# Query loads in halves, key pieces that skip three slots and a later raw block, in a block-sparse attention and MLP kernel

## The chip, the cores and the metric

The kernel runs on one core of a Trainium2 chip. The metric is the time of one execution in microseconds (us), as the median over runs. PE is TensorE's matmul side and PEld its weight loads, DVE is VectorE, ACT is ScalarE, POOL is GpSimd, and SP is SyncE, which here only issues DMAs. "SPq" and "POOLq" are the sides of SP and POOL that issue. A KB of the profile is 1024 bytes; a kB here is 1000.

## The reference

Four batches of eight heads, 768 tokens in 24 blocks of 32, head size 64. Each block of queries sees its own block, its two neighbours, the first and the last block, and three sampled blocks; the first and the last block of queries see everything ("dense"). The result goes through a two-layer MLP.

```python
scores = scale * np.matmul(q, k.transpose(0, 1, 3, 2))
mask = np.abs(blk_i - blk_j) <= 1
mask = mask | (blk_i == 0) | (blk_j == 0) | (blk_i == n_blocks - 1) | (blk_j == n_blocks - 1)
for qb in range(n_blocks):
    for kb in sampled_blocks[qb]:
        mask[qb * block:(qb + 1) * block, kb * block:(kb + 1) * block] = True
scores = np.where(mask, scores, -1000000000.0)
attn = softmax(scores)
x = np.matmul(attn, v)            # reshaped to 3072 tokens x 512
r = np.maximum(x @ w_in, 0.0)     # 512 -> 2048
out = (s * (r * r) + b) @ w_out   # 2048 -> 512
```

## The kernel before, in words

**Attention (about the first 245 us).** Batches 0 and 1 form pair 0, batches 2 and 3 pair 1. The list `T["ORD"]` gives 'slots' in the order of the work. Pair 0 begins with four dense slots (0 to 3); then three streams take turns, C, A and B: slot 4 is the first of C, 5 of A, 6 of B, 7 the second of C, and so on. C walks blocks 17 to 22, A blocks 1 to 8, B blocks 16 down to 9. Pair 1 does the same after four more dense slots that are strewn among the last slots of pair 0. A sparse slot handles one block of queries for all heads of two batches. On PE it is 64 score matmuls (`s`, line 953), 8 transposes of the probabilities (`t`, line 1010), 64 products with the values (`xs`, line 1062), and two transposes of the result (line 1074); every third slot adds products for the dense rows (`od`, line 1052). DVE takes maxima (line 970), ACT the exponentials (line 982).

**What a slot loads.** SP issues the slot's window values (`vA`, line 781) and its three sampled values (line 875), 128 KB each, and stores the result of an earlier slot (`xd<-xst`, line 1086). POOL copies the window's key block and the three sampled key blocks from the pair's key tile `kt` into the work tile `kk` (lines 892 and 903); it does so three slots ahead, as soon as PE has read the stream's previous slot.

**Queries.** A query tile `qr` holds four blocks of queries of two batches, 512 KB, and comes in four DMAs of 128 KB: `load_q` (line 712), two for each batch `a`. A stream changes tile after four slots. In the trace they are called qr_4s and qr_5s (C), qr_0s and qr_1s (A), qr_3s and qr_2s (B) for the sparse slots of either pair, and qr_0d for the dense slots. POOL issues the sparse ones between its key copies; SP issues the dense ones. Four tiles are held at a time.

**Keys of pair 1.** They come in 12 pieces (`key_piece`, `load_k`, line 695), 256 KB each, one right behind the sampled values of each of the slots 9 to 20 (`"K1": 9`).

**Weights.** `w_in` and `w_out` come as 64-bit words and are decoded on DVE, ACT and POOL (lines 85 to 95). The first six blocks (`T["WL"]`: i0 o0 i1 o1 i2 i3) are loaded in two halves of 256 KB each (lines 59 and 62) and decoded during the attention of pair 1; their due time is `wat`, 14 units apart, where a sparse slot has four units.

**What sets the order.** Every step is registered with a cost, a due time and what it needs (`op`). `Plan.order` then lays the steps out on a modelled time axis, with a modelled DMA queue, and the program is written in that order, engine by engine. So a change of due times or of explicit predecessors (`order=`) can move other steps too. On the chip each engine runs its own list in that order.

**MLP (from about 246 us).** PE multiplies without a break: line 617 and the lines 438 to 440 (first layer), 480 to 482 (second).

The lines that the change touches: the table `T` (line 29), `queries` (lines 1160 to 1173), the branch for sparse slots (1181 to 1195), the key pieces (1214) and `wat` (1348).

Of the kernel before, what the change touches and what calls it, by code (L numbers as in the profile page):

```python
# [212 lines left out]
def kernel(  # L213
# [31 lines left out]
    KPS = (4, 12)  # L245
# [415 lines left out]
    with ExitStack() as es:  # L661
# [467 lines left out]
        def key_piece(e, a, p, prio, order=()):  # L1129
            nonlocal prev_k  # L1130
            prev_k = op("s", 450, prio, lambda: load_k(e, a, p), alloc=[] if p or a else [(f"kt{e}", e)],
                        use=[(f"kt{e}", e)] if p or a else [], order=[prev_k, *order], nbytes=3146e3 / KPS[e] / (1 if e else 2))
            for y in range(2) if a is None else (a,):
                kld[(e, y, p)] = prev_k
# [15 lines left out]
        first_pk = first_q = pq = pvl = pvs = pk = o_m = o_e = o_rc = o_ev = None  # L1150
        spills, tensor, lqs, before, globs = {}, {}, {}, {}, {}

        costs = {"s": (530, 470, 265), "d": (810, 350, 780)}
        cols = {"s": (1800, 1024, 500), "d": (1536, 768, 768)}
        for i, (kind, e, k, r) in enumerate(slots):
# [3 lines left out]
            qk = q_of(i)  # L1159
            def queries():  # L1160
                nonlocal pq, first_q
                if qk in lqs:
                    return
                if not dense:
                    first_q = first_q or qk
                lqs[qk] = {}
                for a in range(2):
                    for par in range(2):
                        fresh = not (a or par)
                        pq = op("s" if dense else "g", 450 if dense else 700, max(u - T["QL"], -18.0 if dense else -4.5) + 0.01 * par + (9.5 * (u == 0) if dense else 0.02) * a,  # L1170
                                lambda qk=qk, a=a, par=par: load_q(qk, a, par), alloc=[("qr", qk)] if fresh else [], use=[] if fresh else [("qr", qk)],
                                order=[pq] if dense else [pq, o_rg if first_q in (None, qk) else first_pk], nbytes=131e3)
                        lqs[qk].setdefault(a, []).append(pq)
# [6 lines left out]
            else:  # L1180
                prev = before.get(r)
                entire = k == STREAMS[r]
                first = not before
# [5 lines left out]
                first_pk = first_pk or pk  # L1189
                queries()  # L1190
                for a in range(NSL):
                    pk = op("g", 460, u - T["GK"] + 0.1 * (a + 1), lambda i=i, a=a: sampled_k(i, a), [o_rg, *parts_of(e, range(NB))],
                            alloc=[] if a else [("kg", i)], use=[(f"kt{e}", e), ("kk", "kk")] + ([("kg", i)] if a else []), order=[pk])
                    s_deps.append(pk)
                s_use += [("kk", "kk"), ("kg", i)]

# [16 lines left out]
                pv_at.append((u, pvs))  # L1213
                if 0 <= i - T["K1"] < KPS[1]:
                    key_piece(1, None, i - T["K1"], u - T["GV"] + 0.4, [pvs])
                av_use = [*vt, ("vs", i)]
# [129 lines left out]
        for k, (which, f) in enumerate((w[0], int(w[1:])) for w in T["WL"].split()):  # L1346
            load, st = decode(which, f, k)
            wat = N + min(T["WP"] + T["WS"] * k, T["WE"] + T["WD"] * k if k < 6 else 1e9)
            raw, wp = ("kraw", (which, f)), (f"wp{quarter_of(k)}", (which, f))
# [218 lines left out]
```

## Time and profile before

| | |
|---|---|
| three runs | 772.94, 774.55 and 776.96 us, median 774.55 us |
| the profiled execution | 772.34 us, its span 770.6 us |
| busy, of the span | PE 732.4 us, DVE 568.1 us, ACT 475.1 us, POOL 242.1 us |
| instructions on PE | 8032 matmuls, 8032 weight loads |
| mean granted clock of PE | 0.986 |
| DMA | 89.14 MB, 116 GB/s over the span |
| key pieces of pair 1 issued | from 44.3 to 95.9 us |

The profile comes from one execution. Its page has busy times by engine, the span in 40 slices, DMA queues, and the chain of work that ended last, followed back from the last instruction. Other views are the waits (who waited for whom: sum, count, longest), stretches ("windows": for each engine the busy time and the count of instructions, then PE's granted clock, the DMA engines' busy share and GB/s), a tile's instructions, and the chain and the timeline in order of time (start, duration, what). "issue" is time in which an engine waited for nothing that the profile shows.

### The profile page before, as it was taken

The page shows a single profiled execution, that of the slowest core. Times are in us where ns is not written, and L with a number is a line of the kernel's source. Part 1 is how long each engine was busy: PE and PEld are TensorE (multiplying, and loading weights), DVE is VectorE, ACT ScalarE, POOL GpSimd, SP SyncE. Part 2 cuts the span into 40 slices and gives each one's busy share as a digit, 9 for nine tenths or more (in the row PEclk, how much of TensorE's full clock was granted, in tenths as well). Part 3 has the DMA queues.
Part 4 walks back from the last instruction along what each step waited for, and adds up shares of the span by engine and source line. Part 5 has one row for each costly group of instructions (what it writes and reads, how often), then busy time and mean ns, then how long its engine had stood idle before and what let it go on. Part 6 is the DMA issues. An engine that isn't in the chain of part 4 may idle for free.

```text
span 770.6 us, 21377 instructions
## 1 busy us (share of the span) xinstructions
PE 732.4 (95%) x8032; PEld 619.7 (80%) x8032; DVE 568.1 (74%) x1437; ACT 475.1 (62%) x1143; POOL 242.1 (31%) x398
## 2 busy tenths in 40 slices
PE   8699898999788999999989999999999999999997
PEld 6377675676567999999878998888998998888896
DVE  4767466988586789897896688687678678667652
ACT  3767576888586878789753444565443567344433
POOL 4936244546230221211022232223222232222221
PEclk9989999999899999999999999999999999999999
DMA  8978888877774534635433222224000022000002
GB/s 237 235 199 223 233 215 223 206 202 213 178 202 117 159 110 148 209 118 161 101 126 90 76 83 75 63 69 123 1 1 1 1 62 83 1 1 0 1 1 82
DMA packets 100998, 89.14 MB, mean 116 GB/s; under 512 B 50208, under 2 KB 79520, under 8 KB 100896
## 3 DMA queue, kind: packets, MB, share of 16 engines
q1 hardware_dynamic: 98592, 81.50, 37.8%
q0 software_dynamic: 2304, 6.29, 3.3%
q8 instruction: 63, 1.03, 0.6%
q14 instruction: 39, 0.32, 0.1%
HBM read 68.89 MB, written 14.68 MB: 108 GB/s over the span
## 4 chain that ended last, share of the span: by engine, by line
PE 75%; DVE 9%; ACT 5%; issue 4%; DMA 3%; POOL 1%; SPq 1%; POOLq 0%; ACTq 0%; DVEq 0%
PE m L617 20%; PE o L481 10%; PE o L482 10%; PE o L480 10%; PE xs L1062 5%; PE s L953 5%; PE t L1010 4%; PE h L438 3%; PE h L440 2%; PE h L439 2%; PE od L1052 2%; DVE ptile L970 1%; PE xs L1074 1%; DMA qr_3s<-in_q_dup_dram 1%; DVE xp L601 1%
## 5 line engine op out<-in xcount | busy, mean ns | idle before, releaser
L459 POOL TENSOR_TENSOR hid<-hid,hid 128x384 fp32r<-128x384 f32 x96 | 105.6, 1101 | 292.3 <-ACT hid L635 245.6
L634 ACT ACTIVATE hid<-hid,sb_b,sb_s 128x384 f32<-128x384 f32 x96 | 68.0, 709 | 151.6 <-DVE hid L628 151.5
L982 ACT ACTIVATE ptile<-ptile,nm 128x256 f32<-128x256 f32 (+1 forms) x208 | 107.2, 518 | 35.3 <-DVE nm L970 35.0
L970 DVE CUSTOM_DVE_ANT_1 ptile<-s,mt 128x256 f32<-128x256 f32 x176 | 64.4, 421 | 33.2 <-PE s L953 32.4
L482 PE MATMUL o<-woutr,hid 128*128 128x512 f32 x168 | 66.4, 395 | 0.0
L481 PE MATMUL o<-woutr,hid 128*128 128x512 f32 x168 | 66.3, 395 | 0.0
L480 PE MATMUL o<-woutr,hid 128*128 128x512 f32 x168 | 65.3, 389 | 0.0
L617 PE MATMUL m<-wout,win 128*128 128x384 f32 x264 | 62.6, 340 | 2.1 <-ACT xrest L1461 1.6
L617 PE MATMUL m<-xp,wop 128*128 128x384 f32 x288 | 58.3, 337 | 0.0
L1062 PEld LDWEIGHTS xs<-vA,pt 128*32 128x32 f32 x1696 | 36.6, 113 | 26.9 <-issue 8.5
L481 PE MATMUL o<-win,hid 128*128 128x512 f32 x144 | 56.8, 395 | 0.0
L628 DVE SCALAR_TENSOR_TENSOR hid<-hid 128x384 f32<-128x384 f32 x96 | 54.3, 566 | 3.3
L1010 PE MATMUL t<-ident,ptile 128*128 128x128 f32 x352 | 51.0, 285 | 5.7 <-issue 5.3
L617 PE MATMUL m<-xp,win 128*128 128x384 f32 x288 | 55.1, 338 | 1.4 <-DVE xp L601 0.7
L1062 PE MATMUL xs<-vA,pt 128*32 128x64 f32 x1696 | 49.0, 228 | 6.5 <-issue 5.3
L617 PEld LDWEIGHTS m<-xp,win 128*128 128x128 f32 x288 | 50.9, 188 | 4.5 <-DVE xp L601 1.2
L635 ACT CAST hid<-hid 128x384 fp32r<-128x384 f32 x96 | 49.4, 514 | 7.5 <-PE o L482 0.4
L617 PEld LDWEIGHTS m<-xp,wop 128*128 128x128 f32 x288 | 51.5, 188 | 2.1
L617 PEld LDWEIGHTS m<-wout,win 128*128 128x128 f32 x264 | 47.4, 188 | 5.1 <-ACT xrest L1461 2.5
L482 PE MATMUL o<-win,hid 128*128 128x512 f32 x126 | 49.8, 395 | 0.0
L892 POOL COPY kk<-kt 128x256 f32<-128x256 f32 (+2 forms) x46 | 21.3, 466 | 90.4 <-PE s L953 90.2
L480 PE MATMUL o<-win,hid 128*128 128x512 f32 x126 | 49.2, 391 | 0.2
(191 smaller groups left out, 1860.6 us busy)
## 6 DMA issues: line engine op xcount, KB each, us to landing
vB<-in_v_dram SPq DMA_DIRECT2D x113, 128.0 KB, 4.1
vA<-in_v_dram SPq DMA_DIRECT2D x73, 128.0 KB, 3.9
raw_o<-in_w_out_dram SPq DMA_DIRECT2D x14, 512.0 KB, 3.4
raw_i<-in_w_in_dram SPq DMA_DIRECT2D x12, 512.0 KB, 3.8
xd<-xst SPq DMA_DIRECT2D x44, 128.0 KB, 3.7
out_dram<-ob SPq DMA_DIRECT2D x20, 256.0 KB, 2.0
sum<-xd SPq DMA_DIRECT2D x12, 384.0 KB, 4.2
kt<-in_k_blk_dram SPq DMA_DIRECT2D x8, 384.0 KB, 5.5
```

Of the source, the lines that this page charges most:

```text
L459: (eng or nc.vector).tensor_tensor(out=htile(5 + i % 3), in0=t, in1=gh.bitcast(F32), op=ALU.subtract)
L480: nc.tensor.matmul(acc, gh[:, tsl], wout(f, 0), start=first, stop=False)
L481: nc.tensor.matmul(acc, gh[:, tsl], wout(f, 1), start=False, stop=False)
L482: nc.tensor.matmul(acc, gl[:, tsl], wout(f, 0), start=False, stop=last)
L617: nc.tensor.matmul(to, w_, x_, start=(c == 0 and k == 0), stop=(c == 1 and k == 2))
L628: vec.scalar_tensor_tensor(out=t, in0=t, scalar=0.0, in1=t, op0=ALU.max, op1=ALU.mult)
L634: nc.scalar.activation(t, t, AF.Identity, bias=sb_b, scale=sb_s)
L635: nc.scalar.copy(gh, t)
L970: nc.vector.tensor_tensor_reduce(out=pt, in0=sp, in1=msk, scale=-scale, scalar=FMAX if g == 0 else nm[:, 0:1], op0=ALU.add, op1=ALU.min, a ...
L982: nc.scalar.activation(pt[:, :w], pt[:, :w], AF.Exp, bias=nms[n][:, last:last + 1], scale=-1.0, accum_out=dns[i][:, g, j:j + 1])
L1010: nc.tensor.transpose(tp[:, (2 * j + c) * P:(2 * j + c + 1) * P], src[:, c * P:(c + 1) * P], ident)
L1062: nc.tensor.matmul(xs[quads[pair]], pt[:, c, quads[pair]], vt[:, a, col:col + D], start=(j == 0 and c == 0), stop=(c == 1), tile_position= ...
```

## The change

Three edits, and what the planner makes of them. First, the query loads of the second tile of streams A and B may come in two halves, one for each batch: `queries` takes the halves it shall load and a predecessor. Second, the 12 key pieces of pair 1 go behind the sampled values of slots 6 to 14 and 18 to 20 instead of 9 to 20, so slots 15, 16 and 17 have none and slots 6, 7 and 8 have one. Third, the due time of weight block number 4 (i2) is 6 units later.

```diff
-    ... "K1": 9, ...
+    ... "K1": (6, 7, 8, 9, 10, 11, 12, 13, 14, 18, 19, 20), ...
...
-            def queries():
+            def queries(which=(0, 1), after=None):
                 nonlocal pq, first_q
-                if qk in lqs:
+                if which[0] in lqs.setdefault(qk, {}):
                     return
...
-                lqs[qk] = {}
-                for a in range(2):
+                for a in which:
...
-                                order=[pq] if dense else [pq, o_rg if first_q in (None, qk) else first_pk], nbytes=131e3)
+                                order=[pq] if dense else [pq, after, o_rg if first_q in (None, qk) else first_pk], nbytes=131e3)
...
                 prev = before.get(r)
+                if qk[2] == 1:
+                    queries((0,), lastk[sorted(lastk)[-2]])
+                    queries((1,), pk)
+                elif qk[2] == 2:
+                    queries((0,), pk)
...
-                queries()
+                if qk[2] != 2:
+                    queries()
...
+                queries((1,), pk)
+                lastk[i] = pk
...
-                if 0 <= i - T["K1"] < KPS[1]:
-                    key_piece(1, None, i - T["K1"], u - T["GV"] + 0.4, [pvs])
+                if i in T["K1"]:
+                    key_piece(1, None, T["K1"].index(i), u - T["GV"] + 0.4, [pvs])
...
-            wat = N + min(T["WP"] + T["WS"] * k, T["WE"] + T["WD"] * k if k < 6 else 1e9)
+            wat = N + min(T["WP"] + T["WS"] * k, T["WE"] + T["WD"] * k + 6.0 * (k == 4) if k < 6 else 1e9)
```

On POOL, at the place where stream B of pair 1 gets its second query tile, before (qr_1s and qr_2s are query tiles, kk<-kt the key copies of one slot, wklp<-raw_o a step of a weight's decoding):

```order
L712 DMA qr_1s<-in_q_dup_dram 64x4x128 x4
...
L712 DMA qr_2s<-in_q_dup_dram 64x4x128 x4
L88 COPY wklp_549<-raw_o_3745 128x512
L892 COPY kk<-kt_753 128x256
...
L892 COPY kk<-kt_753 128x256
```

and the same place now:

```order
L712 DMA qr_1s<-in_q_dup_dram 64x4x128 x4
...
L712 DMA qr_2s<-in_q_dup_dram 64x4x128 x2
L88 COPY wklp_551<-raw_o_3745 128x512
L892 COPY kk<-kt_465 128x256
...
L712 DMA qr_2s<-in_q_dup_dram 64x4x128 x2
L892 COPY kk<-kt_465 128x256
```

Two of the four loads of qr_2s stand behind the key copies of one more slot. The four of qr_1s stand together as they did. Pair 0 shows the same two changes, and its four loads of the next qr_4s now stand together, behind the copies of slot 21, where three stood behind those of slot 22 and one behind those of slot 23.

On SP, early in pair 0, behind the sampled values of slot 6 (vA, vB are value tiles, kt the key pieces), before:

```order
L875 DMA vB<-in_v_dram 32x2x512
L781 DMA vA<-in_v_dram 96x2x512
L872 DMA vB<-in_v_dram 32x2x512
L875 REGISTER_ALU
```

and now:

```order
L875 DMA vB<-in_v_dram 32x2x512
L695 DMA kt_465<-in_k_blk_dram 128x2x256
L781 DMA vA<-in_v_dram 96x2x512
L872 DMA vB<-in_v_dram 32x2x512
L875 REGISTER_ALU
```

A key piece stands ahead of the next value loads; two more follow behind slots 7 and 8. Later on SP, the three pieces behind slots 15, 16 and 17 are gone, and three of the four loads of qr_0d for pair 1's dense slots move forward by one to two slots, so that three of them now stand among the key pieces of slots 18 to 20.

On SP, in pair 1, around the halves of weight block i2 (raw_i, lines 59; xd<-xst stores one slot's result, so that its rows count the slots), before:

```order
L59 DMA raw_i_4064<-in_w_in_dram 128x2x256
L1086 DMA xd<-xst_4060 128x256
...
L59 DMA raw_i_4064<-in_w_in_dram 128x2x256
L1086 DMA xd<-xst_4158 128x256
...
L1086 DMA xd<-xst_4252 128x256
...
L1086 DMA xd<-xst_4375 128x256
```

and now:

```order
L1086 DMA xd<-xst_4060 128x256
...
L1086 DMA xd<-xst_4156 128x256
...
L59 DMA raw_i_4238<-in_w_in_dram 128x2x256
L1086 DMA xd<-xst_4252 128x256
...
L59 DMA raw_i_4238<-in_w_in_dram 128x2x256
L1086 DMA xd<-xst_4373 128x256
```

Both halves come two slots later. The steps that decode this block move later with them on DVE, ACT and POOL. PE's own list is the same before and now.

More of the change, by code (lines that the diff above doesn't have):

```diff
@@ L1150 @@
         first_pk = first_q = pq = pvl = pvs = pk = o_m = o_e = o_rc = o_ev = None
-        spills, tensor, lqs, before, globs = {}, {}, {}, {}, {}
+        spills, tensor, lqs, before, globs, lastk = {}, {}, {}, {}, {}, {}
         costs = {"s": (530, 470, 265), "d": (810, 350, 780)}
```

2 rows, old and new, of the table T are left out of this document.

## The prediction

> **What bounds the kernel now.** I read the page first. PE is busy for 95% of the span and carries three quarters of the chain that ended last, so PE's stops are what can be won.
>
> ```profile
> PE 732.4 (95%) x8032; PEld 619.7 (80%) x8032; DVE 568.1 (74%) x1437; ACT 475.1 (62%) x1143; POOL 242.1 (31%) x398
> PE 75%; DVE 9%; ACT 5%; issue 4%; DMA 3%; POOL 1%; SPq 1%; POOLq 0%; ACTq 0%; DVEq 0%
> q8 instruction: 63, 1.03, 0.6%
> ```
>
> Stretches tell where PE stops. In the MLP it does not: 40.00 us busy out of 40. So what is won in the attention comes off the end one for one, as long as the weights keep ahead.
>
> ```profile
> 260.00:300.00 40.00, 40.00 (x202) 36.25 (x201) 34.83 (x65) 31.73 (x58) 8.14 (x9) 1.00 0.37 111
> ```
>
> PE's waits in the first 280 us (sum, count, longest) show two kinds that matter: "issue", where PE waits for nothing that is recorded, 10.7 us in two rows, and the queries qr_3s at the start.
>
> ```profile
> PE xs L1062 <- issue: 5.4, 8, 2.8
> PE t L1010 <- issue: 5.3, 2, 4.6
> PE s L953 <- DMA qr_3s<-in_q_dup_dram: 5.0, 2, 3.5
> PE xs L1074 <- DVE xss L1068: 3.3, 3, 1.8
> ```
>
> The chain in order of time (start, duration, what) puts the "issue" stops at two places, at 76 to 85 us and at 197 to 201 us. Work on PE right behind the long ones is slow: 1.89 us for the 32 scores that take 1.02 us elsewhere.
>
> ```profile
> 75.86 2.83 issue
> 78.69 0.87 PE xs L1062 x45
> 79.56 1.32 PE t L1010 x8
> 81.31 1.89 PE s L953 x32
> 83.20 0.86 PE xs L1062 x39
> 84.07 1.18 issue
> 88.12 1.02 PE s L953 x32
> 89.15 1.08 PE xs L1062 x62
> 91.31 1.02 PE t L1010 x8
> ...
> 92.55 1.02 PE s L953 x32
> ...
> 196.78 4.59 issue
> 201.38 0.90 PE t L1010 x3
> 202.71 1.89 PE s L953 x32
> 204.59 1.86 PE xs L1062 x64
> ```
>
> What are these stops? Both stand inside a run of equal instructions, so no operand is late. The page has 63 packets of instructions, 1.03 MB: 16 kB each, and one for every 255 of PE's 16064 instructions, which is about one a slot. I read the stops as PE's next block of program coming late. No view shows one packet's time; that is inference. What speaks for it is what the DMA engines do there:
>
> ```profile
> 70.00:77.00 7.00, 5.86 (x166) 4.14 (x164) 5.70 (x26) 5.63 (x21) 7.00 (x15) 1.00 0.85 220
> 77.00:86.00 9.00, 6.12 (x159) 4.23 (x161) 2.98 (x13) 4.27 (x16) 2.33 (x7) 0.81 1.04 258
> 192.00:196.00 4.00, 3.88 (x132) 2.86 (x131) 3.86 (x12) 3.44 (x13) 2.13 (x5) 1.00 1.07 234
> 196.00:200.00 4.00, 0.78 (x9) 0.53 (x5) 2.03 (x10) 1.23 (x6) 0.33 (x2) 0.95 1.06 255
> 204.00:210.00 6.00, 6.00 (x172) 4.54 (x160) 3.10 (x12) 3.88 (x13) 1.45 (x5) 0.80 0.28 78
> ```
>
> At both places they are full (the share before GB/s is 1.04 to 1.07); behind the second, 0.28. The four query loads of qr_2s go out at just these places (the first at 74.1 us, the last of pair 1 at 189.5), and they land late; qr_4s, loaded in a calmer place, lands in 4.2 us at the median, qr_2s in 7.6. Landing rows of the two tiles, qr_2s first, min/median/max:
>
> ```profile
> L712 POOL DMA_DIRECT2D qr_2s<-in_q_dup_dram x8: 615/615/730, 74.1 to 189.5; - x8
> DMA to landing us min/median/max: 7.0/7.6/8.6
> ...
> DMA to landing us min/median/max: 3.4/4.2/4.9
> ```
>
> So about 7.6 - 4.2 = 3.4 us of transfers stand in line there (up to 4.4), and a block of program stands behind them too. A backlog of 3.4 us gave a stop of 2.83 us: a stop is about the backlog less 0.6 us.
>
> **The change, part by part.** *Key pieces out of slots 15 to 17.* Before, pieces went out all through the first place:
>
> ```profile
> 66.49 0.42 SPq L695 DMA_DIRECT2D kt<-in_k_blk_dram  x1
> ...
> 70.72 0.64 SPq L695 DMA_DIRECT2D kt<-in_k_blk_dram  x1
> ...
> 74.73 0.45 SPq L695 DMA_DIRECT2D kt<-in_k_blk_dram  x1
> ...
> 80.64 0.40 SPq L695 DMA_DIRECT2D kt<-in_k_blk_dram  x1
> ```
>
> The last three are those of slots 15 to 17: 3 x 262 = 786 kB, at the 220 to 258 GB/s of these stretches 3.3 us. The second half of qr_2s, 262 kB, 1.1 us, comes one slot later. Together 4.4 us leave a backlog of 3.4 to 4.4 us. What comes in: three loads of qr_0d (393 kB, 1.6 us) move forward among the key pieces of slots 18 to 20, at 85 to 93 us. So there I expect stops of 1.6 - 0.6 = 1.0 us and of half that in the slot behind, 1.5 us in all, short enough for PE to keep its clock, as it did after the 1.18 us at 84.07 (1.02 us for the scores at 88.12). What goes is 2.83 + 1.18 us of stops, and the slow work: 0.30 (transposes, 1.32 against 1.02), 0.87 (scores), 0.27 (45 and 39 products in 0.87 and 0.86, where 62 take 1.08 at 89.15): 5.4 us. Net -3.9 us. Bounds: all of it goes, -5.4; or the cluster makes one stop as long as the longest seen, 4.59 us with its 2.2 us of slow work, +1.4 against now.
>
> A page of the Trainium skill speaks against this reading. "Runtime: NRT & Kernel Launch", section "Instruction fetch mechanics", says that program comes in blocks of 16 KiB, 256 instructions, over the sequencer's own DMA queue while the present block runs, and that the cost of a boundary is mostly hidden. The size agrees with the packets here; by "mostly hidden" this edit would save nothing and the sum would keep only its costs. The stops of 2.83 and 4.59 us beside full DMA engines make me hold with the rows.
>
> *Key pieces to slots 6 to 8.* The same 786 kB now come between about 27 and 38 us. The stretches there:
>
> ```profile
> 27.00:34.00 7.00, 3.82 (x52) 2.19 (x49) 6.78 (x22) 5.25 (x19) 7.00 (x14) 1.00 1.05 252
> 34.00:38.00 4.00, 1.46 (x16) 0.41 (x16) 0.63 (x3) 1.81 (x6) 2.72 (x8) 0.72 1.04 236
> 38.00:42.00 4.00, 4.00 (x85) 2.19 (x82) 2.07 (x10) 1.01 (x3) 1.71 (x5) 0.50 0.53 126
> ```
>
> PE stands still here for qr_3s, 5.0 us in the waits above, and this wait is on the path. The first piece goes out ahead of qr_3s: 262 kB at 252 GB/s, 1.0 us later. The second goes out behind qr_3s, since a group of sampled values lies between, and the third falls to the stretch with 0.53 of the engines busy. I take +1.0 us. Upper end, all three ahead of qr_3s: 3.1 us. Below 0 nothing speaks for a gain, since bytes are only added. PE's clock is at 0.50 behind the wait as it is, so a longer wait should not cost it again. The value loads behind the pieces come up to 3 us later too; PE's slot 6 needs them only after slots 4 and 5.
>
> *qr_2s of pair 1 in halves, block i2 later.* The second place, on SP:
>
> ```profile
> 187.05 0.41 SPq L59 DMA_DIRECT2D raw_i<-in_w_in_dram  x1
> ...
> 191.83 0.41 SPq L59 DMA_DIRECT2D raw_i<-in_w_in_dram  x1
> ```
>
> These two halves, 524 kB or 2.2 us at 234 to 255 GB/s, leave by two slots, and half of qr_2s, 1.1 us, by one. The backlog, at most 8.6 - 4.2 = 4.4 us, falls to 1.1 us, a stop of 0.5 us. Two slots on, the raw halves come where the stretch 204 to 210 us has engines at 0.28 (partly because PE had stood); I add 0.5 us for them. What goes: 4.59, and 0.52 (three transposes in 0.90, at 1.02 for eight), 0.87 (scores), 0.75 (64 products in 1.86, by the same measure 1.11): 6.7 us. Net -5.7 us. Bounds: -6.7; or 0, if the stop only moves with the raw block.
>
> The half of qr_2s is issued one slot later and still lands before its use: PE reads it about three slots, 13 us, after the copies that it follows.
>
> *Decoding of i2.* Its nine steps move two slots towards the end of the attention, where PE already waits for DVE three times, 3.3 us (the xss row above). DVE is in order, so a decode step ahead of a maximum or of xss delays PE. +0.6 us, between 0 and the 1.8 us of the longest such wait. The MLP needs i2 as its fifth piece, so it isn't late there.
>
> *qr_4s of pair 1.* Its four loads come a little earlier, four issues of 0.6 us ahead of slot 22's key copies, which run three slots ahead: nothing.
>
> **The sum.** -3.9 + 1.0 - 5.7 + 0.6 = -8.0 us. The profiled execution took 772.34 us, 2.2 us below the median of the three runs. 772.34 - 8.0 = 764.3; on the scale of the median 774.55 - 8.0 = **766.5 us**. Ends of the forecast's own case: all stops gone and no cost, 774.55 - 12.1 = 762.4; half the gain lost, 770.5.
>
> **The rivals.** About 0.5%, 3.9 us, is what a measurement can tell from no change: 770.7 to 778.4.
>
> *A, the first place only changes its slot.* Three loads of qr_0d, two key pieces and nine value or result transfers come in two slots of 4.4 us (88.12 to 92.55), 393 + 524 + 1180 = 2.1 MB in 8.9 us: 236 GB/s, about what full engines move here, and qr_4s comes on top. For: 70 to 77 us looked like that before. Against: the backlog starts from less. Then the first edit gives nothing: 1.0 - 5.7 + 0.6 = -4.1, 770.5 us.
>
> *B, the second stop moves with the raw block.* The bytes stay; they meet another block of program two slots later. -3.9 + 1.0 + 0.6 = -2.3, 772.3 us. Against: no query load is near by then.
>
> *C, the stops aren't a matter of load, so the change doesn't do what it is laid out for.* A block of program has its own queue and waits for nobody, and the stop has its place in the program: all stay, 774.55 + 1.0 + 0.6 = 776.2 us. For: no view shows the packet. Against: three stops, all beside full engines.
> Such a rule stands in the Trainium skill, "DMA: Bandwidth & Descriptors", "Queues, rings and completion order": each DMA engine takes the queues in turn, a packet at a time, so a block would wait for one packet of each. No run yet shows the turns.
>
> *D, slower: the start pays in full and gets nothing back.* All three pieces go ahead of qr_3s at 27 to 37 us, +3.1, and the cluster at 85 to 93 us makes the long stop, +1.4, with B's +0.6 and nothing won in pair 1: 774.55 + 5.1 = 779.7 us. It decides if qr_3s lands over 2.5 us later than now and backlog simply goes where the bytes go. For: the bytes are the same. Against: pieces two and three go out behind qr_3s.
>
> **How the numbers follow.** Forecast 0.58, A 0.20, B 0.08, C 0.08, D 0.06. Faster by over 0.5% needs below 770.7 us: nearly all of the forecast's case (0.57) and A's better part (0.13): 0.70. Within 0.5%: the rest of A, B and C, 0.24. Slower: D, 0.06. The range runs from 762.0, all stops gone, to 774.5: A and B lie in it, and C, D and a little below 762 stay out, under 0.2.
>
> **What would show it.** Right: no "issue" stop over 1.5 us on PE between 70 and 82 us and none over 1 us behind 185 us, scores at 1.02 us there, landing of qr_2s near 5 us, PE's wait for qr_3s about 6 us, the MLP starting about 8 us sooner. The first edit is wrong if a long stop stands at 83 to 95 us. The reading as a whole is wrong if the stops stay at the same instructions while the engines have room, or if "issue" shrinks and the MLP starts no sooner because PE waits for DVE or a transfer in its place.

## The result, and the profile after

The changed kernel took 767.8 us (median of 20 runs) where the kernel before took 773.05 us (20 runs beside it). The ratio is 0.9936, with a 95% interval from 0.9914 to 0.9959: 4.9 us faster, between 3.2 and 6.6. Timed a second time it came to 0.9959 (0.9931 to 0.9987), 3.2 us. The profiled execution took 766.6 us, its span 764.8 us (770.6 before).

The page of the profile after, busy times and the chain's shares:

```profile
PE 731.6 (96%) x8032; PEld 619.3 (81%) x8032; DVE 567.7 (74%) x1437; ACT 475.1 (62%) x1143; POOL 243.0 (32%) x398
PE 73%; DVE 7%; issue 6%; ACT 5%; DMA 4%; POOL 3%; POOLq 0%; SPq 0%; ACTq 0%; DVEq 0%
```

PE's busy time hardly moved (732.4 to 731.6 us); what is gone is idle time. PE's waits in the first 280 us (sum, count, longest):

```profile
PE xs L1062 <- issue: 7.0, 8, 2.0
PE s L953 <- DMA qr_3s<-in_q_dup_dram: 4.0, 2, 2.8
PE xs L1074 <- DVE xss L1068: 2.5, 3, 1.7
```

The row with one stop of 4.6 us in the transposes is gone. But "issue" in the products went up, from 5.4 to 7.0 us. The chain in order of time shows where. First place:

```profile
55.81 0.99 issue
...
70.14 0.52 issue
...
75.01 0.39 issue
...
79.55 2.03 issue
81.58 1.19 PE xs L1062 x45
82.77 1.90 PE t L1010 x8
...
85.09 1.16 PE s L953 x32
...
95.41 0.59 issue
95.99 0.87 PE xs L1062 x47
96.87 1.02 PE t L1010 x8
97.89 0.22 PE xs L1074 x2
98.11 1.02 PE s L953 x32
99.13 0.69 PE xs L1062 x38
99.82 1.08 issue
```

The stop of 2.83 us is still there, as 2.03 us, at the same product (45 of 64 behind it), with half-rate work behind it. The one of 1.18 us is gone, and small ones of 0.39 to 1.08 us have come, from 55 to 100 us. The second place:

```profile
195.59 0.70 PE t L1010 x5
196.29 0.61 issue
196.91 0.55 PE t L1010 x3
...
197.67 1.02 PE s L953 x32
...
200.63 0.73 issue
```

Here 4.59 us have become 0.61, at the same transpose (five ahead of it, three behind), and the work behind runs at full rate: 0.55 us for three transposes where it was 0.90, 1.02 for the scores where it was 1.89. Stretches of the changed kernel, columns as before:

```profile
77.00:86.00 9.00, 6.97 (x148) 5.12 (x146) 4.11 (x16) 4.75 (x16) 4.07 (x9) 0.81 0.92 265
...
196.00:200.00 4.00, 3.38 (x115) 2.35 (x115) 2.99 (x15) 2.64 (x10) 1.14 (x4) 1.00 0.86 242
204.00:210.00 6.00, 6.00 (x204) 4.72 (x204) 5.60 (x24) 5.27 (x17) 2.15 (x5) 1.00 0.62 185
260.00:300.00 40.00, 40.00 (x202) 36.16 (x201) 36.38 (x66) 32.27 (x59) 7.47 (x9) 1.00 0.46 143
```

The second place gave load to 204 to 210 us (0.28 to 0.62 of the engines). The first place moves as many bytes as ever, 265 GB/s where 258 stood. The MLP is still one unbroken run of PE. The tile qr_2s now lands sooner, 7.6 to 5.3 us at the median:

```profile
L712 POOL DMA_DIRECT2D qr_2s<-in_q_dup_dram x8: 617/617/617, 77.2 to 191.2; - x8
...
DMA to landing us min/median/max: 5.0/5.3/6.3
```

(A slot has 32 score matmuls in these traces, not 64 as the section on the kernel before says.)

### The profile page after: what moved, and what is told of

It is laid out like the page before. It is cut to its first block, busy times and chain, and to the rows that moved or that the text cites. A ratio compares the mean times of both kernels' runs of the same rounds, so it can differ in the third digit from the quotient of the medians.

```text
span 764.8 us, 21376 instructions
## 1 busy us (share of the span) xinstructions
PE 731.6 (96%) x8032; PEld 619.3 (81%) x8032; DVE 567.7 (74%) x1437; ACT 475.1 (62%) x1143; POOL 243.0 (32%) x398
## 4 chain that ended last, share of the span: by engine, by line
PE 73%; DVE 7%; issue 6%; ACT 5%; DMA 4%; POOL 3%; POOLq 0%; SPq 0%; ACTq 0%; DVEq 0%
PE m L617 20%; PE o L481 10%; PE o L482 10%; PE o L480 10%; PE xs L1062 5%; PE s L953 4%; PE t L1010 4%; PE h L438 2%; PE h L440 2%; PE h L439 2%; PE od L1052 2%; DMA qr_3s<-in_q_dup_dram 1%; POOL kk L903 1%; PE xs L1074 1%; DVE xp L601 1%
## 5 line engine op out<-in xcount | busy, mean ns | idle before, releaser
L903 POOL COPY kk<-kt 128x256 f32 x132 | 50.0, 417 | 0.0
```

The source lines that it names most:

```text
L903: nc.gpsimd.tensor_copy(flat(kg[:, a:a + 1]), flat(kts[e][:, bass.ds(j, 1)]))
```

## The experiments

The theory: PE stops where its next block of program is due, and a stop is long when the DMA engines have a backlog there. Rivals: the stops belong to the work and not to load (C of the prediction); the gain is made somewhere else than at the two places.

PE runs the same list in all these kernels, so a matmul can be found again by its number among the 8032 (of the work, in the shifted kernels). The table gives what each trace gained or lost against the trace of before, from the start of one numbered matmul to another in the timelines: the 161st to the 361st (24.5 to 43.5 us in the trace of before), to the 2001st (103.8), the 2701st (134.9), the 4101st (190.1), the 4401st (208.7), the 5301st (240.3) and the 8001st (758.1). "Timed" is the ratio of the timed runs (20 runs in the first row, 9 or 12 in the others); "own" is how far the profiled execution lies from its kernel's median. All columns from "own" on are us.

| kernel | timed | own | start | pair 0 | between pairs | pair 1 to 190 | 2nd place | end of attention | MLP |
|---|---|---|---|---|---|---|---|---|---|
| changed | 0.9936 (0.9914 to 0.9959) | -1.2 | 1.5 | 1.7 | -4.4 | 1.1 | **-5.3** | -0.6 | 0.6 |
| changed, again | 0.9959 (0.9931 to 0.9987) | -5.1 | 1.3 | 0.6 | -3.9 | -0.6 | **-5.0** | -0.8 | -0.1 |
| keys alone | 0.9981 (0.9957 to 1.0006) | 1.0 | 0.5 | -1.1 | 0.3 | 0.0 | 0.0 | -0.1 | 0.4 |
| halves alone | 1.0008 (0.9984 to 1.0033) | -0.8 | 1.5 | 1.8 | -3.6 | 0.2 | **-2.3** | 1.7 | 0.4 |
| raw block alone | 0.9986 (0.9966 to 1.0007) | 1.8 | 0.7 | 1.1 | -3.9 | 3.9 | **-1.4** | 0.7 | -0.2 |
| keys, halves | 1.0004 (0.9975 to 1.0032) | -1.7 | 0.9 | -0.2 | -3.9 | 3.3 | **-2.3** | 0.0 | 0.0 |
| keys, raw block | 0.9971 (0.9945 to 0.9998) | 1.1 | 0.1 | 2.2 | -3.9 | 0.0 | **-2.5** | 0.7 | -0.2 |
| halves, raw block | 0.9974 (0.9951 to 0.9997) | -3.6 | -0.4 | 2.7 | -3.9 | 1.3 | **-4.7** | -0.9 | 0.0 |
| halves, raw, keys 8 to 14, 18 to 22 | 0.9977 (0.9955 to 0.9999) | 1.9 | 1.4 | 1.8 | -1.1 | 1.6 | **-4.0** | -0.1 | 0.5 |
| before, 21 loads left out | 0.9925 (0.9898 to 0.9951) | 0.5 | 0.8 | -1.2 | -0.5 | -0.5 | **-5.5** | 0.8 | 0.0 |
| before, blocks shifted | 1.0086 (1.0061 to 1.0112) | -0.7 | -2.4 | 4.1 | -3.6 | 3.7 | -1.5 | -0.1 | 1.7 |
| changed, blocks shifted | 1.0004 (0.9978 to 1.0030) | -5.0 | -4.9 | -0.7 | -2.0 | 3.7 | -6.1 | 1.8 | 1.1 |

Only the second place, and in part the end of the attention, order themselves by the edits. The start, pair 0, the stretch between the pairs and pair 1 up to 190 us scatter by 2 to 5 us whatever was changed, and single executions lie up to 5 us off their median. How much of that is mere scatter can be read off: up to 187 us the later raw block moves no DMA and no compute step, so the rows without it and with it are the same program up to there. Two such rows differ by up to 1.9 us at the start (1.5 and -0.4, with halves), 3.3 in pair 0 (-1.1 and 2.2, with keys), 4.2 between the pairs (0.3 and -3.9, with keys) and 3.9 up to 190 us (0 and 3.9, before and raw block alone). So a term is read from a stage in several traces, and the time from the timed runs.

**One edit at a time.** Keys alone, against before (the code that follows the tuple is that of the change):

```diff
-    ... "K1": 9, ...
+    ... "K1": (6, 7, 8, 9, 10, 11, 12, 13, 14, 18, 19, 20), ...
```

> The kernel before with the key pieces alone moved (slots 6 to 14 and 18 to 20); queries and raw blocks as before. Theory, one: a stop of PE's program follows the backlog of transfers. The pieces then cost 1.2 us at the start, bring nothing over the first place (the load only changes its slot), and win about 4 us in the dense slots of pair 1 (111 to 132 us), because the three loads of qr_0d that they pull forward leave the engines free for the values and the raw block: ratio about 0.997 to 1.000 (-2.5 to 0 us), the stop of 4.59 us at 197 us stays within 1 us. Rival, the 4 us in the dense slots were an accident of one execution: +2 to +4 us, 1.003 to 1.005. Rival, the prediction's own term (first place -3.9, start +1.0): -2.9 us, with no stop over 1.5 us between 70 and 82 us.

Measured: -1.5 us, the interval from -3.3 to +0.5 us. The stop of the second place is as long as before, at the same transpose:

```profile
196.24 5.00 issue
201.24 0.90 PE t L1010 x3
```

Three of the four loads of qr_0d move forward with this edit alone. The 4 us between the pairs did not come with it, so that part of the theory falls. The prediction's own -2.9 is inside the interval; a trace that shows it there is lacking: at the first place 2.03 us of stop were left at 78.97 us.

Halves alone: the change without the tuple and the last edit.

```diff
+                if qk[2] == 1:
+                    queries((0,), lastk[sorted(lastk)[-2]])
+                    queries((1,), pk)
+                elif qk[2] == 2:
+                    queries((0,), pk)
...
+                queries((1,), pk)
+                lastk[i] = pk
```

> The kernel before with the query loads in halves alone (qr_2s of both pairs: two loads, and two more a slot later); key pieces and raw blocks as before. Load theory: 262 kB, 1.1 us, leave each of the two backlogs, so the stop of 2.83 us falls to about 1.7 and the one of 4.59 us to about 3.5; with the half-rate work shorter or gone -2 to -5 us, 0.994 to 0.997. Rival, the stops are not a matter of load: same places, same lengths within 0.3 us, 0 us.

Measured: +0.6 us (-1.2 to +2.5), which leaves out the theory's -2 to -5 us of time. The stops of the second place did shrink, to 0.89 and 1.44 us, and the stage won 2.3 us; but at the end of the attention 1.7 us came back. In this trace PE's granted clock is 0.50 from 214.9 to 218.3 us, behind a wait of 1.8 us for DVE that the trace of before has as well, with the clock at 1.00 behind it; so the 1.7 us are not shown to be a price of the halves. The first place had stops of 1.48 and 3.66 us, more than before.

The raw block alone:

```diff
-            wat = N + min(T["WP"] + T["WS"] * k, T["WE"] + T["WD"] * k if k < 6 else 1e9)
+            wat = N + min(T["WP"] + T["WS"] * k, T["WE"] + T["WD"] * k + 6.0 * (k == 4) if k < 6 else 1e9)
```

> The kernel before with the raw block i2 alone two slots later. Load theory: 2.2 us leave the second backlog, the stop of 4.59 us falls to 2 to 2.5 us, and with part of the half-rate work -2 to -5 us; given back at the end of the attention up to 1.4 us: ratio 0.994 to 0.999. The first place (2.83 + 1.18 us at 76 to 85 us) does not change. Rival, the stop moves with the raw block to 203 to 213 us: 0 to +1 us, 1.000 to 1.002. Rival, not a matter of load: the 4.59 us stay.

Measured: -1.1 us (-2.6 to +0.5). The chain has the two places:

```profile
77.05 2.03 issue
82.90 3.93 issue
...
198.67 2.95 issue
201.62 0.90 PE t L1010 x3
```

The second stop went from 4.59 to 2.95 us, with half-rate work behind it, and no stop came up two slots on. The first two rows teach something else: up to 185 us SP and POOL run the very program of before here, and the stops there are 2.03 + 3.93 us where the trace of before has 2.83 + 1.18. That much an execution differs from the next.

Halves and raw block, the key pieces back at slots 9 to 20:

```diff
-    ... "K1": (6, 7, 8, 9, 10, 11, 12, 13, 14, 18, 19, 20), ...
+    ... "K1": tuple(range(9, 21)), ...
```

> The changed kernel with its key pieces put back (slots 9 to 20): halves and the later raw block alone. Theory: the second place brings 5 to 6 us whatever the key pieces do, the first place 1 to 2 us for the half of qr_2s, with 0.6 to 1.4 us given back at the end: -4.5 to -7 us, 0.991 to 0.994, so it is as fast as the changed kernel or faster by up to 2 us. Rival, the key pieces carry part of the gain (the dense slots): -2 to -4 us, 0.995 to 0.997, slower than the changed kernel.

Measured: -2.0 us (-3.8 to -0.2): the theory's -4.5 is outside, the rival's -2 to -4 fits. The trace shows the second place as in the changed kernel (1.44 and 0.73 us, three transposes in 0.55), but it is of an execution 3.6 us under the median. At the first place it has stops of 2.58 and 2.50 us, so the half of qr_2s won nothing there.

Between the pairs this kernel, with its keys at the old slots, has the 3.9 us too. DVE's waits from 110 to 140 us name what was there before; first the trace of before, then keys alone:

```profile
DVE wkhp L85 <- DMA raw_i<-in_w_in_dram: 2.5, 1, 2.5
```

```profile
DVE wkhp L85 <- DMA raw_i<-in_w_in_dram: 0.9, 1, 0.9
```

With halves and raw block, and in the changed kernel, there is no such row; but the raw block alone has one of 1.1 us and keys with raw block one of 1.4, and both have the 3.9 us all the same. The 4 us go with neither keys, halves nor raw block: they are there without each, and in the kernel with shifted blocks, which has none of the edits (3.6 us). The raw block alone runs the program of before in this stretch. So they are a bad moment of the one execution that was profiled of before; how often it has them stays open (keys alone and the kernel without 21 loads hardly win anything there either).

**Pairs of edits.** Keys and halves, the raw block in its old place:

```diff
-            ... T["WE"] + T["WD"] * k + 6.0 * (k == 4) if k < 6 else 1e9)
+            ... T["WE"] + T["WD"] * k if k < 6 else 1e9)
```

> The changed kernel with the raw block i2 at its old place: key pieces and halves of the queries alone. Load theory: 2.2 us of transfers come back to the second place, the stops at 192 to 201 us are 2 to 3.5 us in sum instead of 1.3, and PE's clock may fall behind the longest: 2 to 4 us slower than the changed kernel, -1 to -3 us against before, 0.996 to 0.999. Rival, the raw block's move does nothing by itself: as fast as the changed kernel, 0.993 to 0.995.

Measured: +0.3 us (-1.9 to +2.5). The stops of the second place were 0.34 and 2.13 us in sum, as the theory had it; its -1 to -3 us of time lies half inside the interval, and the rival falls. Keys and raw block, the queries in one piece (the diff of the halves undone):

> The changed kernel with the query loads in one piece again: key pieces and later raw block alone, the last of the eight combinations. Theory, the raw block's move is what the gain hangs on, and the halves add a little: the stop at 197 us is 2.5 to 3.5 us as with the raw block alone (2.95), -2 to -4 us against before, 0.995 to 0.998, 1 to 3 us slower than the changed kernel. Rival, the halves do nothing: 0.993 to 0.996, as the changed kernel. Rival, the halves carry it: 0.998 to 1.001.

Measured: -2.2 us (-4.2 to -0.2). The stop at 195.98 us was 3.08 us, as with the raw block alone.

The eight combinations together: with the raw block moved the time is lower in all four pairs (by 0.14, 0.34, 0.10 and, with the two measurements of the changed kernel averaged, 0.57%), 0.29% or 2.2 us at the mean. The halves win in the two pairs that have the raw block moved (0.12 and 0.24%) and lose in the two that have not (0.08 and 0.23%). The keys win 0.19, 0.04, 0.15 and 0.26%, 1.2 us at the mean, where one such difference is uncertain by 0.3%: that they bring anything is likely, not settled.

**The key pieces elsewhere.** No early pieces at the start, two later ones instead:

```diff
-    ... "K1": (6, 7, 8, 9, 10, 11, 12, 13, 14, 18, 19, 20), ...
+    ... "K1": (8, 9, 10, 11, 12, 13, 14, 18, 19, 20, 21, 22), ...
```

> The changed kernel with its key pieces behind slots 8 to 14 and 18 to 22 instead of 6 to 14 and 18 to 20: nothing goes out early at the start, two pieces go out later. Theory: the 1.2 us of the start go away (PE's wait for qr_3s ends as before), the place of slots 15 to 17 stays as in the changed kernel: 0.5 to 1.5 us faster than the changed kernel, -5.5 to -6.5 us against before, 0.991 to 0.993. Rival: the two pieces behind slots 21 and 22 come late for the dense slots of pair 1 at about 113 us, or swell the backlog there: 1 to 4 us slower than the changed kernel.

Measured: -1.8 us (-3.5 to -0.1), 1.4 us behind the changed kernel run beside it, which is within the uncertainty; the 0.5 to 1.5 us that the theory promised aren't there. (One piece, behind slot 8, still goes out a slot earlier than before, at 39.31 us; PE's wait for qr_3s is over by then.) The start took 1.4 us more than in before, without any piece ahead of that wait. So the 1.5 us of the changed kernel at the start aren't shown to be a price of the pieces.

**The changed kernel again**, unchanged:

> The changed kernel itself once more, beside the others on the same chip. If the edits add up, keys alone and halves with raw block gave -1.5 and -2.0 us, so -3.5 us, 0.9955; if they need each other, -5 us, 0.9935 as at first. The profile of a second execution tells which of the stops come again: theory, stops stand at the same matmuls (the 1349th, five transposes into the slot at 196 us for the 4257th), but their lengths differ by up to 2 us from one execution to the next.

Measured: -3.2 us (-5.3 to -1.0). Its stops at the first place were 1.48 us at 77.69 and 2.08 us at 83.00 us, at the second 1.31 and 0.46 us: the same products and transposes, other lengths. The time is what the parts add up to, -3.5 us; the -4.9 us of the first timing are not excluded by it.

**Are the stops blocks of program?** First try, 64 matmuls of 8 columns in the first warm-up step:

```diff
                 nc.tensor.matmul(box["warm"][:, :P], ident, ident, start=True, stop=True)
+            if n == 4 and "more" not in box:
+                box["more"] = 1
+                for _ in range(64):
+                    nc.tensor.matmul(box["warm"][:, :8], ident, ident[:, :8], start=True, stop=True)
```

> The kernel before with 64 tiny matmuls (8 columns each) more in the first warm-up step, while PE waits for its first data anyway: nothing else changes, but every later matmul stands 64 places on in PE's program, half of the 127 that lie between two stops. Theory, the stops are PE's next block of program: they move 64 matmuls up in the work. None at the 20th of 64 products (slot at 76 us) nor at the sixth transpose at 197 us; instead stops at the 1285th or 1412th matmul of the work, and at the 4193rd or 4320th. Rival, the stops belong to the work (an operand, a semaphore, a queue): they stay at the 1349th and the 4257th matmul of the work. The time: within 4 us of before either way, since the blocks meet the same load at other moments.

Measured: 1.0270 (1.0233 to 1.0306). It decided nothing. In fp32 the 64 are 128 records, one whole block, so all stops stood where they had, and the 128 took 27 us of PE. Second try, in bf16:

```diff
-            for _ in range(n):
+            for _ in range(n if n == 2 else 1):
                 nc.tensor.matmul(box["warm"][:, :P], ident, ident, start=True, stop=True)
+            half = ident.bitcast(BF16)
+            for _ in range(22 if n == 4 else 0):
+                nc.tensor.matmul(box["warm"][:, :8], half[:, :P], half[:, :8], start=True, stop=True)
```

> The kernel before with 88 tiny bf16 matmuls (8 columns) in place of 12 of the 24 warm-up matmuls, which the profile counts twice each: PE has 64 records of matmuls more ahead of the work, half of the 127 between two stops (the 64 tiny ones tried before were fp32, counted as 128, just one block, and took 27 us). Theory, the stops are PE's next block of program: they move 64 matmuls up in the work; none longer than 0.4 us at the 20th product of the slot at 76 us nor at the sixth transpose at 197 us (in the work the 1349th, 1475th and 4257th matmul), stops at the 1285th, 1412th, 4193rd or 4320th instead. Rival, they belong to the work and stay. The time: -4 to +4 us against before, as the blocks meet the same load at other moments.

Measured: 1.0086, 6.6 us slower (4.7 to 8.6), outside the -4 to +4 that was expected. The chain of this kernel at the first place:

```profile
75.09 1.02 PE xs L1062 x62
76.11 0.93 issue
77.04 0.30 PE xs L1062 x2
...
79.61 1.03 PE xs L1062 x64
...
81.94 0.56 PE s L953 x8
82.51 1.28 issue
83.79 1.07 PE s L953 x24
...
86.97 0.91 PE t L1010 x7
87.88 2.84 issue
...
91.52 1.89 PE s L953 x32
```

Two products are left behind the first stop, not 45. The full run of 64 products at 79.61, which had the 2.83 us, has none, nor have the transposes of the second place; there the stops are 1.57 and 4.00 us, in the products of two slots. By their number in the work they lie at 1287, 1413, 1540, 4067 and 4194. Three of them are 63 or 64 from the old stops at 1350, 1476 and 4258; the other two are 63 from the next places in that row, 1603 and 4130, the second of which was a stop with halves alone (the expectations count from 0). The stops went with the position in PE's program. Rival C's half, that they have their place in the work, falls.

The distance can also be counted in the fences above: 47 + 8 + 2 + 32 + 38 = 127 matmuls from 95.41 to 99.82 us in the changed kernel, 254 instructions with their weight loads, and 256 with the two semaphore instructions that the trace has of PE in between. The Trainium skill, "Runtime: NRT & Kernel Launch", section "Instruction fetch mechanics", gives 256 instructions to a block; the traces agree. That the cost of a boundary is mostly hidden, as it says there, holds for most of the 63 blocks here, but not at the two places.

**Are they long because of load?** The kernel before without the loads of sampled values of seven slots around the two places:

```diff
-            nc.sync.dma_start(out=vt[a * BLK:(a + 1) * BLK], in_=...)
+            if nth[i] not in (10, 11, 12, 13, 34, 35, 36):
+                nc.sync.dma_start(out=vt[a * BLK:(a + 1) * BLK], in_=...)
```

> The kernel before without 21 loads of sampled values, 131 kB each, those of slots 14 to 17 (1.57 MB, issued at about 66 to 80 us) and of the sparse slots 42 to 44 (1.18 MB, 185 to 197 us); their products use the values of an earlier slot, all other work is the same. Load theory: without the backlog no stop over 0.6 us is left at 70 to 86 us and at 192 to 201 us, PE keeps its clock there, and the kernel comes 5.4 + 6.7 us sooner by the prediction's terms, less up to 2 us for the end of the attention: -9 to -12 us, 0.984 to 0.988. Rival, the stops are not a matter of load: 4.0 and 4.6 us of them stay, and the time changes by less than 2 us.

Measured: -5.8 us (-3.8 to -7.9), about half of what the theory gave. Stretches of this kernel:

```profile
70.00:77.00 7.00, 7.00 (x226) 5.20 (x224) 5.79 (x24) 5.75 (x20) 6.61 (x15) 1.00 0.60 173
77.00:86.00 9.00, 6.01 (x198) 4.81 (x199) 4.98 (x23) 5.01 (x18) 3.87 (x10) 0.95 0.99 222
...
196.00:200.00 4.00, 3.45 (x125) 2.52 (x126) 3.69 (x17) 3.29 (x12) 1.43 (x4) 1.00 0.44 121
```

and its chain at the two places (the lines stand two lower in this kernel):

```profile
77.42 1.18 issue
...
82.43 1.80 issue
...
84.77 1.66 PE od L1054 x32
86.44 1.90 PE t L1012 x8
...
199.61 0.71 issue
```

At the second place the load is down to under half of the engines, and of the 4.59 us 0.71 are left, at the next block; at the old transpose there is none. At the first place stops of 1.18 and 1.80 us are left, and the load too: in spite of 1.57 MB less the engines are full at 77 to 86 us, share 0.99 (222 GB/s where 258 stood). SP simply came sooner to what stands behind. Its key pieces from there on go out at 64.31, 67.95, 73.40 and 76.91 us, where they went out at 66.49, 70.72, 74.73 and 80.64. Stops stayed where load stayed and went where it went.

**The packets of program.** No view lists single packets, but the kept traces hold them, and they settle what the prediction had to infer. In the trace of before, PE entered the block ahead of the 4.59 us stop at 193.30 us (the end of the last matmul before it); the packet of 16384 bytes with the next block started only at 198.90 us, took 1.06 us and was done at 199.96, and PE went on at 201.38. In the changed kernel PE entered at 192.81, the packet started at 194.39 and was done at 195.58, and PE went on at 196.91. The 14 traces have 131 stops over 0.3 us at the end of a block in the first 245 us, and every one ends 1.25 to 1.73 us behind the end of such a packet.

The packet itself takes about as long beside idle engines as beside full ones; what load delays is its start. All blocks between 40 and 245 us, in 13 traces (without the fp32 filler):

| share of the DMA engines in the 1.5 us behind PE's entry into the block ahead | packets | start behind that entry, median (us) | packet, median (us) | stops over 0.8 us |
|---|---|---|---|---|
| under 0.3 | 39 | 0.55 | 0.97 | 0 |
| 0.3 to 0.6 | 48 | 0.75 | 1.16 | 1 |
| 0.6 to 0.9 | 273 | 1.55 | 1.08 | 20 |
| 0.9 and more | 171 | 2.39 (at most 7.5) | 1.14 | 34 |

So the load theory holds over all blocks and not only at the two places. Which transfers a late packet stands behind is not recorded.

**Change and shift together**, the edit of the warm-up in the changed kernel:

> The changed kernel with the 64 matmuls more ahead of the work, as in the kernel with 88 tiny matmuls in the warm-up, which was 6.6 us slower than before. Theory, the change works by taking load out of the second place, wherever the blocks of program lie: the stops of 1.57 and 4.00 us at 191 to 201 us shrink to under 2 us together and the scores and transposes behind them keep 1.02 us; against the shifted kernel -3 to -5.5 us, so +1 to +4 us against before, 1.001 to 1.005; the first place keeps its 4 to 7 us of stops. Rival, the gain hung on where the blocks happened to lie: as slow as the shifted kernel, 1.007 to 1.010. Rival, more of the first place's gain shows here, since more stops lay there: -6 us or better against the shifted kernel, under 1.001.

Measured: 1.0004, so 0.9919 of the shifted kernel, -6.3 us (-3.5 to -9.1 with both intervals). The theory's -3 to -5.5 and the rival of more gain at the first place, -6 or better, both lie within that interval, the number itself with the rival. In the traces the second place won 4.6 us against the shifted kernel and pair 0 4.8, the latter in an execution 5.0 us under its median. The second place, in which 1.57 and 4.00 us had stood, now has:

```profile
186.79 1.02 issue
...
191.64 1.53 issue
```

That is 2.55 us together, where the theory had under 2. At the first place, where it had 4 to 7 us left, three stops of 0.48 to 0.71 us stand in place of 0.93, 1.28 and 2.84: so one execution of these blocks did win there. The gain doesn't hang on where the blocks happened to lie.

## Why the prediction was right, and where it was not

It forecast -8.0 us; measured were -4.9 and -3.2. The time lies inside the stated range, but that range takes in rivals A and B, and -8.0 itself lies outside both intervals. The number nearest to the measured ones is rival A's, -4.1, and broadly for its reason: the second place gave what it should, the first little. Of the signs it named, qr_2s landed in 5.3 us and no stop over 1 us was left behind 185 us (1.31 in the second trace); but 2.03 us stood at 79.55 us, PE's wait for qr_3s was 4.0 us and not about 6, and the MLP began 6.3 us sooner (the sum of the changed kernel's columns up to it, with the 0.3 us ahead of the 161st matmul), not 8.

*The reading of the stops* held: blocks of program, late beside full engines. The rule of thumb, backlog less 0.6 us, did not: the halves take 1.1 us of transfers out of the second place and bring its stops from 4.59 to 2.33 us (2.47 with the keys), the raw block takes 2.2 us and brings them only to 2.95 (3.08 with the keys). That suggests, from two traces each, that it counts which transfers stand ahead of the block, not their sum alone.

*First place, -3.9*: this step failed. "Together 4.4 us leave a backlog of 3.4 to 4.4 us" sets transfers that go out over 10 us (70.72 to 80.64) against a backlog of one moment, and so takes all stops there for gone. The packet of the block that came late started 3.8 us behind PE's entry into the block ahead (72.05 to 75.87) in the trace of before, and 4.0 us (75.01 to 79.01) in the changed kernel. The six traces with the pieces out of slots 15 to 17 (the shifted kernels and the one with loads left out aside) have pair 0 0.8 us slower than the trace of before at the mean (-1.1 to +2.2), the four with the pieces there 1.4 us (0, 1.8, 1.1, 2.7). The difference, -0.6 us, is less than what either group scatters. Split in two it says more. From the 969th to the 1729th matmul (63.7 to 94.2 us in the trace of before), which holds the place, the six are 0.7 us faster than that trace at the mean (-1.8 to +0.8) and the four 1.6 us slower (0 to +2.2); from there to the 2001st the six are 1.3 us slower (-0.4 to +2.4) and the four 0.1 us faster (-0.8 to +0.5). So some 2.3 us are won at the place, not 5.4, and 1.4 us come back right behind it, where qr_0d now goes out among the key pieces: the 1.5 us that the prediction had for that. Before and after, the engines move about 260 GB/s at 77 to 86 us; what SP has next fills most of the room, as the kernel without 21 loads shows. And the step took 2.83 + 1.18 us of one execution for a property of the kernel, where another execution of the same stretch of program had 2.03 + 3.93. In the second execution of the changed kernel 2.08 us stood at 83.00 us, which is the sign that the prediction named for this.

*The start, +1.0*: the changed kernel lost 1.5 us there, but four kernels without pieces ahead of qr_3s lost 1.5, 0.7, 1.4 and -0.4. PE's wait for qr_3s did not grow to 6 us; it was 4.0. A price of the early pieces is not shown.

*Second place, -5.7*: right. The four unshifted traces with halves and raw block won 5.3, 5.0, 4.7 and 4.0 us there, 4.8 at the mean; one edit alone won 1.4 to 2.5, the key pieces 0.0. It takes both, as the step had it.

*Decoding of i2, +0.6*: the sign was wrong by a little. One wait of PE for DVE, 1.8 us at 215 us before, is gone with the later block, and 1.1 us come back in two waits behind it (0.4 us are new at 221 us of the changed kernel, 1.1 became 1.7 at 226). The stage gave -0.6, -0.8, -0.9 and -0.1 us with both edits. With the raw block moved and the queries in one piece it was +0.7, twice; there the granted clock was 0.50 for 3.4 us behind the longer wait.

*The sum.* 4.8 + 0.6 (the mean of the four) = 5.4 us show stage by stage; the timed runs say 4.9 and 3.2, 2.0 for halves and raw block without the keys and 1.8 with the keys elsewhere, with some 2 us of uncertainty on each. Three of those four traces are of executions under their median, so they promise a little more than the mean execution gives. Whether the keys bring their 1.2 us stays open. The two profiles differ by 5.7 us as well, but through other terms: -4.4 us between the pairs, which come without the change too, and +4.3 us that were lost at the start, in pair 0 and up to 190 us, of which no edit can be shown to be the cause.

*The rivals.* B fell: where the raw block went, no stop over 0.73 us came up. C fell with the shifted blocks and the loads left out; the rule of the Trainium skill that it named ("DMA: Bandwidth & Descriptors", "Queues, rings and completion order"), queues taken in turn by packet, would let a block through quickly; beside full engines its packet started up to 7.5 us behind PE's entry into the block ahead, and PE stood up to 5.00 us. What the turns are is not recorded. D fell: no price at the start is shown, and pair 1 gained.

## What to carry to other kernels

A stop of PE inside a run of equal instructions, with no releaser and at a fixed distance in its program from other such stops, was here its next block of program; it was long where the DMA engines were full, so thinning the loads around that spot can win more than their time. It wins only if nothing queued behind moves up into the room: look at what the issuing engine does next, and take transfers to where the engines stand idle, not to the next full slot. The packets of the program's queue, where a trace keeps them, show such a stop directly. A term read from a stall of one profiled execution should be given the spread that two executions show there, here 2 us and more.

## What the runs showed of the hardware that was not expected

- PE's next block was fetched one block ahead at most: its packet started when PE entered the block ahead or later (from 0.7 us before that entry to 7.5 us behind it), took about 1.1 us, and at the stops PE went on 1.25 to 1.73 us behind its end. A block of the attention lasted 3.8 us where nothing stopped it (95.99 to 99.82 us in the changed kernel), so by estimate, from these three figures, a start over 1.4 us behind the entry stopped PE.
- Where the blocks of program lie seems to cost time by itself: 64 more matmuls ahead of the same work made the kernel before 6.6 us slower. Its stops over 0.3 us at the ends of blocks sum to 16.8 us in the first 245 us, where before has 10.4, the changed kernel 9.2 and 7.5, and the kernel without 21 loads 5.3. That the warm-up itself was changed too was not separated from it.
- An fp32 matmul of 8 columns is no cheap filler: 64 of them are 128 records and took 27.3 us, 0.21 us each, with 27.4 us of weight loads beside them; 88 of the same width in bf16 took 3.1 us.

```profile
L1108 PE MATMUL warm<-ident 128*128 128x8 f32 x128 | 27.3, 360 | 0.0
```

```profile
L1107 PE MATMUL warm<-ident 128*128 128x8 bf16 x88 | 3.1, 170 | 0.0
```

- Work ran at half rate behind every stop of 2.83 us and more, and at full rate behind 1.18, 1.44 and 1.53 us. In between the length doesn't decide: half rate came behind 1.80 us (without 21 loads) and 2.03 us (changed kernel), and full rate behind 1.80 us (keys and raw block), 2.03 us (keys alone, raw block alone) and 2.50 us (halves and raw block, granted clock 1.00). In the kernel with halves alone 0.89 us was enough (64 products in 1.86 us behind it), with 0.40 us of waiting for DVE that ends 1.0 us ahead of it.
